# Batch 0's q and k loaded through GpSimd's queue, zero fills cut to what is read, and a redrawn instruction order, in a linear-attention and MLP-mixer kernel

## The chip, the cores and the metric

The kernel runs on one core of one Trainium2 chip. The metric is the device time of one execution in microseconds. The kernel before takes 242.99 us (median of 3 runs, 242.88 to 243.49).

## The reference, cut to what matters

Eight batches of 576 tokens, 8 heads of 64 (512 channels). Linear attention is followed by a mixer over tokens and one over channels; the result has the residual added.

```python
phi = lambda x: np.where(x > 0, x, np.exp(x) - 1.0) + 1.0
q_p, k_p = phi(q), phi(k)                        # (8, 8, 576, 64)
kv  = einsum('bhsd,bhse->bhde', k_p, v)
z   = sum(k_p, axis=2)
num = einsum('bhsd,bhde->bhse', q_p, kv)
den = einsum('bhsd,bhd->bhs', q_p, z)[..., None] + 1e-06
x   = (num / den) as (8, 576, 512)
h   = relu(x.T @ w_tok1) @ w_tok2                # 576 -> 256 -> 576, per channel
u   = x + h.T
out = u + relu(u @ w_ch1) @ w_ch2                # 512 -> 1536 -> 512, per token
```

Inputs and output are float32.

## The kernel before

**Tiles and stages.** The batches are worked one behind the other, with neighbours overlapped. A batch is loaded as two halves (heads 0 to 3 and 4 to 7) of q, k and v, each 576 KB. For each half ScalarE makes the exp (`phi_exp`, L249), VectorE the linear part (`phi_add`, L253) and the minimum of the two (`phi_end`, L259), which is phi in bf16. TensorE multiplies k and v (`kv`, L299 for batches 1 to 7; `kv_first`, L570 for batch 0), ScalarE copies the result into the block-diagonal tile `kvbd` (L305, L574), q comes to TensorE transposed (by TensorE for batches 0 and 1, `qtr_mm`, L317; by a DMA transpose on SP's queue for the others, `qtr_dma`, L332), and a product with `kvbd` gives numerator and denominator together (L349, L384; `nd_first`, L585 and L592, for batch 0). VectorE divides (L361, L410, L419; L607 for batch 0). Then come the token mixer (`mm1`, L445 and L624; `mm2`, L456, L475, L635), VectorE's residual sum u (L467, L480, L637), u's transpose (on TensorE, or by DMA on SP's queue, L486, L491), and the channel mixer: for batch 0 and part of batch 1 plain products (L683, L744), for the rest a Strassen-Winograd form of seven products, each in 2 by 2 blocks (`mix_mm`, L925, read by L938, L940, L678; `product`, L967, read by L1055, L1061, L981), with sums of blocks on VectorE (L833, L882, L894) and GpSimd (L813, L1068). The tails of 64 tokens that 576 leaves over 512 are worked in pairs of batches (L708, L730, L1021).

**Order.** The order is written out by hand of a planner: every step is a function in a table `tok`, and the string `ORDER` calls them one by one. A name is the batch, then a letter for the step, then its part: `1K` is `kv` of batch 1, `2qT0` a transpose of batch 2's q, `A..` the steps of batch 0, `..L..` a load. Each engine and each DMA queue carries out its own instructions in that order, and waits on semaphores where it reads what another has made. `BANK` says which PSUM bank a product writes, `EBUF` which of three buffers an exp goes to; a bank or buffer that is used again waits for its last reader.

**Queues.** `load` (L221) sends batch 1's halves to GpSimd's queue and all others to SP's. GpSimd's queue also has v of batch 0, cast to bf16 on its way (`load_v0`, L230), all weights, also cast (L1118 to L1137), and the stores of batches 0 to 6. The stores of batch 7 go from SP and ScalarE.

**The beginning.** TensorE multiplies zeros (`warm`, L1089, "the dummy products") while the first loads come in; `zeros` lies in the tile of batch 1's v. Around the loads stand the zero fills: `qT[b]` is the transposed q of two alternating batches, of which the last columns of each quarter and the last 64 are read beyond what is written; `w1t` holds the last 64 rows of w_tok1 in one half of its partitions, for even and for odd batches, and zeros in the other.

```python
js = slice(2 * c, 2 * c + 2)
queue = nc.gpsimd if n == 1 else nc.sync
return after(queue.dma_start(out=raw[nm, rb(n)][:, js], in_=src_[:, js]), gate)
```

Of the kernel before, what the change touches and what calls it, by code (L numbers as in the profile page):

```python
# [43 lines left out]
BANK = {k_: int(v_) for k_, v_ in (e.split(":") for e in """2K:2 2n0:1 2n1:3 2n2:6 2f:6 2g0:4 2g1:6 2X2:1 2Z2:7 2Y2:7 3K:4 3n0:4 3n1:6 3n2:0 3f:4 3g0:6 3g1:0 3X2:1 3Z2:4 3Y2:3  # L44
3gt:2 4K:0 4n0:0 4n1:2 4n2:6 4f:4 4g0:4 4g1:0 4X2:2 4Z2:1 4Y2:3 5K:6 5n0:1 5n1:3 5n2:5 5f:5 5g0:5 5g1:3 5X2:4 5Z2:5
5Y2:7 5gt:1 6K:2 6n0:1 6n1:3 6n2:5 6f:2 6g0:5 6g1:2 6X2:4 6Z2:0 6Y2:6 7K:2 7n0:2 7n1:4 7n2:6 7f:2 7g0:0 7g1:2 7X2:3
7Z2:6 7Y2:1 7gt:5 1h00:2 1h01:1 1h10:6 1h11:5 1t0:3 1t1:2 1t2:1 1t3:6 1m0:2 1m1:4 1m2:3 1m3:4 1m4:6 1m5:2 1m6:4 1m7:1
1m8:0 1m9:5 1m10:0 1m11:0 T00:1 T10:3 T01:4 T11:4 T02:5 T12:7 U08:2 U18:3 7c0:3 7c1:4 7c2:4 7c3:6 7c4:2 7c5:4 7X0:5
7Z0:4 7Y0:1 7X1:2 7Z1:0 7Y1:0 7PX0:7 7PZ0:3 7PY0:1 7PX1:6 7PZ1:5 7PY1:5 7tX:0 7tZ:4 7tY:2 1PX:3 1PZ:0 1PY:2 2PX:4
2PZ:3 2PY:5 3PX:0 3PZ:3 3PY:4 4PX:7 4PZ:0 4PY:0 5PX:0 5PZ:7 5PY:1 6PX:7 6PZ:1 6PY:6 warm0:0 0Q00:1 0Q01:2 0s0:3  # L50
warm1:0 0Q10:7 0Q11:1 warm2:5 0K0:2 0d0:1 0n0:4 0l0:6 0s1:0 0K1:1 0d1:7 0n1:0 0l1:3 0f0:2 0f1:5 0g00:0 0g01:3 0g10:4
0t0:1 0t1:6 0g11:7 0m0:6 0m1:0 0t2:1 0t3:7 0m2:1 0m3:2 0gt:5 0m4:7 0m5:3 0m6:4 0m7:2 0m8:7 0m9:1 0m10:0 0m11:5 U00:3
U01:0 1Q0:5 U02:4 U03:7 1Q1:1 1K:5 1n00:1 1n01:5 1n10:5 1n11:5 1n20:1 1n21:1 1f:5 1g2:0 0ut:6 2X1:0 2Z1:7 2Y1:3 3X1:0
3Z1:3 3Y1:6 4X1:7 4Z1:0 4Y1:0 5X1:6 5Z1:0 5Y1:2 6X1:5 6Z1:6 6Y1:1 2X0:6 2Z0:2 2Y0:2 3X0:2 3Z0:4 3Y0:5 4X0:1 4Z0:7
4Y0:5 5X0:1 5Z0:5 5Y0:0 6X0:7 6Z0:3 6Y0:2""".split())}
# [14 lines left out]
1v1 1Qc10 1K 1Kc0 1Kc1 1Q11 0q3 1Qc11 1n01 1n20 0q4 1nc01 0q5 1n10 1nc20 2Lq1 0q6 1nc10 1n00 1nc00 0q7 1n11 2qx0 2Lv0  # L70
2qx1 2Lk0 2Lk1 0q8 ws04 ws14 2Lv1 1nc11 ws24 ws34 1n21 1nc21 2qa0 2qb0 0q9 2qa1 wt2 1f1 1f0 0q10 1fr1 0q11 2v0 2qb1
3Lq0 2qT1 2qT0 1fr0 1h00 0z0 1h01 0z1 1hu01 1h11 1h10 1hu00 1t0 1hu10 1hu11 1t1 ws00 1g2 1tc1 1t2 1t3 1tc0 1ma9 0z2
1ma5 1ma1 1tc2 1tc3 1mb5 ws10 3qx0 1mb1 1ma2 1mb2 3Lq1 1gu2 2ka1 1ma8 0ut 1r5 1mb8 2kx1 2kx0 1ma7 1r1 3Lk1 1r2 2kb1
1ma0 1mb0 G14 2v1 1r0 0uc 1ma3 1mb3 1r3 2ka0 1mb7 1r7 2kb0 2K 2Kc1 3qa0 2Kc0 1ma4 1mb4 1r8 1r4 0z3 1mb9 1r9 3qb0 ws12
ws22 3qa1 3Lk0 2n 2nd 2o0 2n1 1ma11 1mb11 1r11 2o1 T02 3Lv1 1ma10 1mb10 1p10 1p11 3kx0 1ma6 3Lv0 1mb6 2ne 2n2 2n0 2f0
0o1 3qx1 3qb1 3ka0 3kb0 1r6 ws20 1w10 1w20 Tr02 T00 4Lq1 ws32 1c0 ws30 T01 4Lk0 1r10 1w13 2f1 3ka1 wt0 3kx1 3kb1 1p20
1p21 Tr01 1w23 3qT0 2fr0 2fr1 2g0 4qa1 2gu0 3v0 2g1 1p50 0o0 2gu1 3v1 1p60 4qx1 1p51 1c2 1p61 3K 3Kc0 1w40 1p30 G24
1p31 3qT1 1w30 4qb1 1eZ 1c1 1eY 1hY 1p71 2uT0 1p70 1eW Tr00 3Kc1 3n 1hW 2uT1 U00 1p41 1p40 3nd 3o0 3ne 3o1 3n1 U01
2x01 U02 3n0 3n2 2x12 4Lv1 1hZ 3f0 1eX 2s1 2x11 2s3 2x21 V0 2x15 2s2 4ka0 2y01 2x02 2x06 4kx0 4kb0 4v1 4Lv0 2s4 3f1
# [1118 lines left out]
```

## Time and profile before

| | us |
|---|---|
| median of 3 runs | 242.99 |
| the profiled execution | 244.04 |
| its span | 242.3 |
| PE busy (TensorE, products) | 233.3 (96%) |
| DVE busy (VectorE) | 214.0 (88%) |
| ACT busy (ScalarE) | 135.7 (56%) |
| POOL busy (GpSimd) | 80.8 (33%) |

All times in what follows are microseconds from the start of the span unless said otherwise; the granted clock of TensorE is 0.999 on average. PE is the row of products, PEld that of weight loads, which go on beside products. A row of waits says which engine waited at which line, for whom, the sum, the number of waits and the longest. A row of the chain gives start, length and what it was. Queue q1 is SP's and ScalarE's, q0 GpSimd's. DMA issues stand on the issuing engine; the transfer itself is not in them.

### The profile page before, as it was taken

The page shows a single profiled execution, that of the slowest core. Times are in us where ns is not written, and L with a number is a line of the kernel's source. Part 1 is how long each engine was busy: PE and PEld are TensorE (multiplying, and loading weights), DVE is VectorE, ACT ScalarE, POOL GpSimd, SP SyncE. Part 2 cuts the span into 40 slices and gives each one's busy share as a digit, 9 for nine tenths or more (in the row PEclk, how much of TensorE's full clock was granted, in tenths as well). Part 3 has the DMA queues.
Part 4 walks back from the last instruction along what each step waited for, and adds up shares of the span by engine and source line. Part 5 has one row for each costly group of instructions (what it writes and reads, how often), then busy time and mean ns, then how long its engine had stood idle before and what let it go on. Part 6 is the DMA issues. An engine that isn't in the chain of part 4 may idle for free.

```text
span 242.3 us, 6371 instructions
## 1 busy us (share of the span) xinstructions
PE 233.3 (96%) x2616; PEld 174.4 (72%) x2616; DVE 214.0 (88%) x389; ACT 135.7 (56%) x224; POOL 80.8 (33%) x92
## 2 busy tenths in 40 slices
PE   7799999999999999999999999999999999999991
PEld 3485445465678678789777887788678868888880
DVE  5889986999999999999999999999999699867661
ACT  4764781678695287428993496548914442347000
POOL 8684306370800620046000620215014900440730
PEclk9999999999999999999999999999999999999999
DMA  6999999999799988897937989594971285143035
GB/s 237 267 204 302 314 296 303 410 171 307 263 291 175 327 208 156 293 160 259 301 108 162 379 270 182 88 294 156 157 141 25 45 176 108 24 103 70 3 91 170
DMA packets 49037, 48.42 MB, mean 200 GB/s; under 512 B 30064, under 2 KB 35568, under 8 KB 49008
## 3 DMA queue, kind: packets, MB, share of 16 engines
q1 hardware_dynamic: 40032, 31.46, 47.7%
...
q8 instruction: 20, 0.33, 0.5%
...
## 4 chain that ended last, share of the span: by engine, by line
PE 86%; DMA 8%; DVE 1%; ACT 1%; issue 1%; SPq 1%; ACTq 0%
PE ps L967 26%; PE ps L925 23%; PE ps L445 6%; PE ps L744 5%; DMA v_raw<-in_v_dram 5%; PE ps L456 4%; PE ps L683 4%; DMA k_raw<-in_k_dram 3%; PE ps L708 2%; PE ps L299 2%; PE ps L730 2%; PE ps L1021 2%; PE ps L384 2%; PE ps L624 1%; PE ps L635 1%
## 5 line engine op out<-in xcount | busy, mean ns | idle before, releaser
L967 PE MATMUL ps<-k_raw,v_raw 128*128 128x256 bf16 x252 | 31.5, 273 | 0.0
L940 ACT COPY v_raw<-ps 128x512 f32<-128x512 f32 x30 | 17.2, 593 | 24.1 <-PE ps L925 18.5
L967 PEld LDWEIGHTS <-cr 128*128 128x128 bf16 x252 | 24.5, 98 | 4.8
L967 PEld LDWEIGHTS <-v_raw 128*128 128x128 bf16 x252 | 24.2, 98 | 3.8 <-issue 0.4
L925 PEld LDWEIGHTS <-swc 128*128 128x128 bf16 x240 | 23.3, 98 | 3.5 <-issue 0.4
L925 PEld LDWEIGHTS <-wc 128*128 128x128 bf16 x216 | 21.1, 98 | 4.0
L678 DVE CUSTOM_DVE_ANT_0 cr<-ps,v_raw 128x512 bf16<-128x512 f32 x30 | 20.0, 683 | 4.3 <-PE ps L925 2.1
L925 PE MATMUL ps<-crt,swc 128*128 128x256 bf16 x180 | 23.4, 273 | 0.0
L249 ACT ACTIVATE e<-q_raw 128x1152 bf16<-128x1152 f32 x16 | 18.7, 1167 | 6.7 <-DMA q_raw<-in_q_dram 6.3
L683 PE MATMUL ps<-uT,wc 128*128 128x512 bf16 x96 | 21.9, 379 | 0.0
L967 PE MATMUL ps<-wc,cr 128*128 128x256 bf16 x168 | 21.6, 273 | 0.0
L1068 POOL TENSOR_TENSOR obuf<-obuf,w 128x512 f32<-128x512 f32 x6 | 7.8, 1294 | 40.3 <-DVE obuf L1061 20.2
L249 ACT ACTIVATE e<-k_raw 128x1152 bf16<-128x1152 f32 x16 | 18.6, 1166 | 3.9 <-DMA k_raw<-in_k_dram 3.9
L1068 POOL TENSOR_TENSOR obuf<-obuf,q_raw 128x512 f32<-128x512 f32 x6 | 8.2, 1374 | 35.6 <-DVE obuf L1061 35.6
L925 PE MATMUL ps<-uT,wc 128*128 128x256 bf16 x144 | 19.7, 273 | 0.0
L1061 DVE TENSOR_TENSOR obuf<-ps,u 128x512 f32<-128x512 f32 x24 | 16.3, 684 | 2.7 <-PE ps L967 2.4
L1068 POOL TENSOR_TENSOR obuf<-obuf,part 128x512 f32<-128x512 f32 x6 | 7.7, 1286 | 27.1 <-DVE obuf L1061 27.1
L410 DVE TENSOR_TENSOR x<-ps,dens 128x768 bf16<-128x768 f32 x18 | 16.5, 937 | 0.0
L683 PEld LDWEIGHTS <-wc 128*128 128x128 bf16 x96 | 9.1, 98 | 9.8
L467 DVE TENSOR_TENSOR u<-ps,x 128x1024 bf16<-128x1024 f32 x12 | 14.5, 1218 | 0.1
L833 DVE TENSOR_TENSOR v_raw<-cr 128x512 bf16<-128x512 bf16 (+3 forms) x24 | 14.5, 617 | 0.0
L445 PE MATMUL ps<-x,w 128*128 128x512 bf16 x56 | 14.4, 379 | 0.0
...
## 6 DMA issues: line engine op xcount, KB each, us to landing
...
```

The source lines that it names most:

```text
L249: nc.scalar.activation(out=ebuf[EBUF[f"{n}{nm}{c}"]], in_=f, func=AF.Exp)
L410: nc.vector.tensor_tensor(out=xv[:, :, rc0:rc0 + 3], in0=nd_tile(n, m)[:, :, k0:k0 + 6, 0:D].rearrange("p i (q a) d -> p i q a d", a=2), i ...
L445: nc.tensor.matmul(out=banks(f"{n}f")[:, mt], lhsT=w1t[:, b, ms] if r == R else w1[:, r, ms], rhs=x[b][:, r, :], start=(r == 0), stop=(r = ...
L467: nc.vector.tensor_tensor(out=u[b][:, rs], in0=banks(f"{n}g{i}"), in1=x[b][:, rs], op=ALU.add)
L678: nc.vector._custom_dve(TENSOR_ADD_SAT, out=o, in0=ps, in1=c, s0=3.4028234663852886e38, s1=0.0)
L683: nc.tensor.matmul(out=bank(f"{n}m{mc}"), lhsT=wc1[:, kj, 128 * mc:128 * mc + 128], rhs=uTj[b][:, kj] if n < 2 - U1 else uT[b][:, :, kj], ...
L833: return engine.tensor_tensor(out=s_[which - 1][:, ks], in0=x_, in1=y_, op=op)
L925: nc.tensor.matmul(out=ps[:, j], lhsT=lhs[:, k_, 128 * j:128 * (j + 1)], rhs=rhs[:, :, k_], start=(first and j == 0 and k_ == 0), stop=(k_ ...
L940: nc.scalar.copy(out={1: c1, 6: c6, 5: c5}[i], in_=ps)
L967: nc.tensor.matmul(out=ps, lhsT=lhs[:, k_], rhs=rhs[:, k_], start=(first and not skip and k_ == 0), stop=(k_ == KH - 1), skip_group_check= ...
L1061: nc.vector.tensor_tensor(out=slots(f"{n}P", 4)[:, d::2, HC[c]], in0=pair_tile(n, "X" if z == "W" else z), in1=u[n % 2][:, d::2, HC[c]], o ...
L1068: nc.gpsimd.tensor_tensor(out=o, in0=o, in1=part[i], op=ALU.add)
```

## The change

Three parts. `load` sends batch 0 to GpSimd's queue as well, and the two loads of batch 0's v are issued right behind, ahead of the identity. The zero fills of `w1t` and `qT` move from GpSimd to VectorE, and `qT` is filled only in five blocks of 64 columns (three in `qT[0]`, two in `qT[1]`) in place of all 2368 of each. And the strings `BANK`, `EBUF` and `ORDER` are replaced: the dummy products' banks and the first nineteen steps of batch 0 stay, with the loads of batch 1 and of the weights behind them; the order from there up to step 1066 and all other banks are new; the last steps are as before.

```diff
     def load(nm, n, c, gate=None):
...
-        queue = nc.gpsimd if n == 1 else nc.sync
+        queue = nc.gpsimd if n < 2 else nc.sync
...
     for c, nms in enumerate(("kq", "qk")):
         for nm in nms:
             tok[f"0L{nm}{c}"]()
+    for c in range(2):
+        load_v0(c)
     make_identity(nc, identity)
     nc.vector.memset(ones, 0.0)
...
     for b in range(2):
         nc.vector.memset(kvbd[b], 0.0)
-    nc.gpsimd.memset(w1t, 0.0)
-    nc.gpsimd.memset(qT[0], 0.0)
-    nc.vector.memset(qT[1], 0.0)
+    nc.vector.memset(w1t, 0.0)
     for c in range(2):
-        load_v0(c)
+        for j in sorted({T * c + T, T * (2 + c) + T, 4 * T}):
+            nc.vector.memset(qT[c][:, D * j:D * (j + 1)], 0.0)
     nc.gpsimd.memset(w2p[:, NT * TD:], 0.0)
...
 ORDER = """A2 A0 A1 A3 ... 1Lv1 1Lv0
-B0 B1 B2 A22 A21 A20 A23 A24 A25 A26 A18 A29 A28 A27 A32 A30 A33 A35 A31 A32l A34 Aw10 A36 A37 Aw01 A38 A39 A40 A43
+B0 B1 B2 A21 A20 A25 A18 A23 A24 A22 A26 A29 A27 A30 A28 A33 A31 A32 A32l A35 A34 A36 A37 Aw10 Aw01 A39 A38 A40 A43
...
```

In the new order, as in the old, batch 1's k-times-v product stands behind the same amount of TensorE's work. Among the differences that the prediction speaks of: `A18`, a copy of q, comes behind batch 0's first k-times-v; the first tail product `7ta1` of the last batch stands later among the last products, the tail's mm3 products `7c0` to `7c5` a little later; batch 6's stores (`6o`) are issued behind the last of them.

More of the change, by code (lines that the diff above doesn't have):

```diff
@@ L42 @@
 WHOLE = {'00', '01', 't0', 't1'}
[L44 to L52, printed above, removed]
@@ L53 @@
-U01:0 1Q0:5 U02:4 U03:7 1Q1:1 1K:5 1n00:1 1n01:5 1n10:5 1n11:5 1n20:1 1n21:1 1f:5 1g2:0 0ut:6 2X1:0 2Z1:7 2Y1:3 3X1:0
-3Z1:3 3Y1:6 4X1:7 4Z1:0 4Y1:0 5X1:6 5Z1:0 5Y1:2 6X1:5 6Z1:6 6Y1:1 2X0:6 2Z0:2 2Y0:2 3X0:2 3Z0:4 3Y0:5 4X0:1 4Z0:7
-4Y0:5 5X0:1 5Z0:5 5Y0:0 6X0:7 6Z0:3 6Y0:2""".split())}
+BANK = {k_: int(v_) for k_, v_ in (e.split(":") for e in """2K:0 2n0:4 2n1:6 2n2:1 2f:4 2g0:5 2g1:0 2X2:0 2Z2:5 2Y2:7 3K:6 3n0:4 3n1:6 3n2:0 3f:5 3g0:2 3g1:6 3X2:2 3Z2:1 3Y2:5
+3gt:6 4K:4 4n0:3 4n1:5 4n2:0 4f:6 4g0:6 4g1:6 4X2:0 4Z2:4 4Y2:3 5K:6 5n0:0 5n1:2 5n2:6 5f:6 5g0:4 5g1:6 5X2:6 5Z2:7
@@ new lines @@
+5Y2:5 5gt:2 6K:6 6n0:4 6n1:6 6n2:0 6f:2 6g0:0 6g1:2 6X2:5 6Z2:1 6Y2:4 7K:0 7n0:0 7n1:2 7n2:5 7f:6 7g0:6 7g1:3 7X2:0
+7Z2:7 7Y2:1 7gt:1 1h00:0 1h01:1 1h10:5 1h11:7 1t0:6 1t1:1 1t2:7 1t3:0 1m0:6 1m1:2 1m2:0 1m3:7 1m4:5 1m5:4 1m6:7 1m7:5
+1m8:1 1m9:3 1m10:6 1m11:0 T00:7 T10:0 T01:4 T11:1 T02:6 T12:1 U08:2 U18:0 7c0:7 7c1:6 7c2:0 7c3:4 7c4:5 7c5:3 7X0:4
+7Z0:0 7Y0:5 7X1:2 7Z1:6 7Y1:3 7PX0:2 7PZ0:0 7PY0:1 7PX1:7 7PZ1:6 7PY1:5 7tX:3 7tZ:0 7tY:4 1PX:3 1PZ:5 1PY:2 2PX:7
+2PZ:1 2PY:2 3PX:4 3PZ:3 3PY:5 4PX:3 4PZ:0 4PY:2 5PX:7 5PZ:5 5PY:4 6PX:6 6PZ:7 6PY:3 warm0:0 0Q00:1 0Q01:2 0s0:3
@@ new lines @@
+warm1:0 0Q10:3 0Q11:2 warm2:5 0K0:0 0d0:6 0n0:0 0l0:7 0s1:4 0K1:3 0d1:5 0n1:2 0l1:6 0f0:4 0f1:0 0g00:2 0g01:3 0g10:7
+0t0:2 0t1:4 0g11:3 0m0:7 0m1:3 0t2:3 0t3:1 0m2:1 0m3:6 0gt:5 0m4:4 0m5:6 0m6:0 0m7:4 0m8:2 0m9:5 0m10:6 0m11:2 U00:7
+U01:4 1Q0:0 U02:2 U03:3 1Q1:0 1K:5 1n00:0 1n01:0 1n10:5 1n11:5 1n20:6 1n21:0 1f:5 1g2:4 0ut:0 2X1:4 2Z1:3 2Y1:3 3X1:3
+3Z1:0 3Y1:5 4X1:1 4Z1:2 4Y1:2 5X1:1 5Z1:2 5Y1:4 6X1:2 6Z1:6 6Y1:0 2X0:1 2Z0:6 2Y0:2 3X0:4 3Z0:6 3Y0:0 4X0:5 4Z0:1
+4Y0:4 5X0:0 5Z0:7 5Y0:7 6X0:3 6Z0:6 6Y0:4""".split())}
@@ L57 @@
 SLOT = {k_: int(v_) for k_, v_ in (e.split(":") for e in """0o0:0 0o1:2 1P:0 V0:4 2P:0 3P:0 V1:4 4P:0 5P:0 6P:0 7P0:4 7t:0 7P1:2""".split())}
-EBUF = {k_: int(v_) for k_, v_ in (e.split(":") for e in """0k0:0 0q0:1 0q1:2 0k1:1 1k0:2 1k1:0 1q0:2 1q1:2 2q0:1 2q1:2 2k0:1 2k1:2 3q0:0 3q1:2 3k0:1 3k1:0 4q1:0 4q0:0 4k0:2
-4k1:2 5k0:2 5k1:0 5q0:1 5q1:2 6k1:0 6k0:1 6q1:2 6q0:0 7k1:1 7k0:2 7q0:0 7q1:1 25378:240970""".split())}
+EBUF = {k_: int(v_) for k_, v_ in (e.split(":") for e in """0k0:0 0q0:1 0q1:2 0k1:1 1k0:1 1k1:2 1q0:2 1q1:0 2q0:1 2q1:2 2k0:1 2k1:0 3q0:2 3q1:0 3k0:1 3k1:2 4q1:1 4q0:1 4k0:2
@@ L62 @@
+4k1:1 5k0:2 5k1:1 5q0:2 5q1:0 6k1:2 6k0:1 6q1:0 6q0:1 7k1:2 7k0:1 7q0:2 7q1:0""".split())}
 YBUF = {k_: int(v_) for k_, v_ in (e.split(":") for e in """0k0:0 0q0:0 0q1:0 0k1:0 1k0:0 1k1:0 1q0:0 1q1:0 2q0:0 2q1:0 2k0:0 2k1:0 3q0:0 3q1:0 3k0:0 3k1:0 4q1:0 4q0:0 4k0:0
@@ L70 @@
[L70 to L79, printed above, removed]
@@ L105 @@
-7cr5 7x23 7w10 7cr4 7x24 7y23 7c3 7y24 7w30 7w20 7c2 7y13 7w14 7c0 7cr2 7w12 7w40 7cr3 7p50 7w34 7cr0 7w22 7p51 7w24
-7w42 7p10 7w44 7ts1 7p11 7ta1 7R11 7R51 7p20 7w32 7t5 7R10 7ts2 7R50 7p61 7tb1 7p31 7R61 7ts4 7R20 7p30 7R31 7tr5 7p60
-7tr1 7ts3 7p71 7R60 7p21 7t6 7R21 7R30 7p70 7R71 7D200 7tr6 7t3 7D711 7D710 7ta2 7D201 7tr3 7D210 7R70 7tb2 7p41 7D311
+B0 B1 B2 A21 A20 A25 A18 A23 A24 A22 A26 A29 A27 A30 A28 A33 A31 A32 A32l A35 A34 A36 A37 Aw10 Aw01 A39 A38 A40 A43
+A41 A42 0gt At3 2Lq0 At2 0ma0 0gv 1ka0 1kx0 1kb0 0ma3 0ma1 0ma4 0mb4 0mb0 1kx1 0mb3 G01 0r3 1ka1 0ma6 1kb1 0ma8 0mb8
@@ new lines @@
+0ma2 0mb2 0mb6 G11 0r8 G21 0r0 G13 G02 0r6 0r4 0ma9 1qx0 G04 G12 0ma10 0mb10 0ma11 0r10 0ma7 0mb7 0mb1 0mb11 0r2 1qa0
+0ma5 1qb0 0mb5 G03 1qa1 0r7 G14 0r1 0mb9 0r9 1Q00 0r11 G22 1qx1 ws02 1Q01 ws04 ws12 1Qc00 0q0 1Qc01 1qb1 1v0 0q1 0q2
+0r5 1Q10 1Qc10 ws22 1v1 1K 1Kc1 1Q11 0q3 1Kc0 1n20 1Qc11 0q4 1n01 1nc20 0q5 1n10 0q6 2qx0 1nc01 1nc10 1n00 1nc00 0q7
+1n11 ws14 0q8 1n21 2Lq1 2qx1 1nc11 1nc21 2qa0 G24 2qb0 2qa1 G23 2qb1 ws00 0q9 0q10 2Lv0 2Lk0 1f0 1fr0 1f1 1fr1 2Lk1
+2Lv1 2v0 3Lq0 3Lq1 0q11 0z0 1h01 1hu01 1h00 0z1 ws24 1h11 1hu11 1h10 1hu00 1t0 1tc0 1t1 2qT0 1hu10 1g2 1t3 2qT1 1t2
@@ new lines @@
+3Lv0 ws10 1tc1 1ma0 1ma4 2kx1 1ma8 1gu2 1tc3 1ma5 1tc2 2kx0 1ma2 1mb2 0z2 ws34 1mb5 1mb8 1ma3 2ka1 2v1 1r2 3Lk1 3qx0
+2kb1 1mb4 3qx1 2ka0 3Lk0 1r8 1mb0 1r0 2kb0 1r4 1mb3 1r3 1ma1 1mb1 3qa0 2K 2Kc1 0z3 1r5 3qb0 2Kc0 0o1 3qa1 1ma7 1mb7
+1r7 1r1 0o0 3Lv1 1ma9 1mb9 1r9 2n 4Lq1 0ut 0uc wt2 1p10 1p11 3kx0 1ma11 1mb11 2nd 2n1 2o1 1ma10 1mb10 1r10 2ne 2o0 2n0
+1ma6 1mb6 1r6 2n2 2f1 3qb1 3qT1 wt0 3ka0 1w10 3qT0 2fr1 1r11 1w13 ws32 2f0 3kb0 T00 4Lk0 2fr0 2g0 3ka1 1w23 1w20 1p50
+1p51 ws20 ws30 2gu0 1w40 3v0 3kx1 3kb1 Tr00 T01 2g1 1w30 1c0 1p61 T02 1c2 1p31 2gu1 3v1 4Lv1 Tr02 1p60 4qx1 1c1 4qa1
@@ new lines @@
+1p20 1p21 1eZ 4qb1 4ka0 1p71 3K 3Kc0 1p30 1eY 1hY 1p70 Tr01 1eW 3Kc1 3n 3nd 3ne 4kx0 U00 4v1 U01 U02 3o1 3n2 3n1 2uT1
+1p41 1p40 1hZ 2uT0 2x21 2y21 3n0 3o0 2s1 1eX 2x01 2x02 2s2 1hW 2y01 2y02 5Lq1 5qx1 4Lq0 2x25 2y25 V0 2x11 2x26 4kb0
+2y11 4qa0 3f0 4qx0 2x12 2x05 2s3 2y12 4qb0 2x06 3f1 2x15 3fr0 4Lv0 2y06 2x07 4Lk1 4ka1 2s4 2y05 5Lk0 3fr1 2y07 2x03
+2x16 2y03 2x22 2y22 2y15 2x23 2y26 2y23 2x27 2y27 2y16 2x13 2y13 4v0 2x17 5kx0 3g1 2x04 3g0 2x24 2y17 2y04 2x14 3gu1
+2w10 4kx1 2p10 2p11 1o 3gu0 2y24 2y14 2w12 2p20 5Lv1 4kb1 3gt 4K 2w22 2c0 2w20 2p21 4qT1 4Kc1 2w30 2p61 2p60 2c1 4qT0
@@ new lines @@
+2eZ 2p50 2p51 2c2 3gt1 4Kc0 3uT1 2p71 3gt0 2p70 3s3 2w40 4n 3uT0 3s1 5Lv0 2p30 2eW 2p41 5v1 2hW 5v0 2p31 4nd 4ne 4o0
+4n0 5Lk1 5kx1 2p40 3x11 3y11 4n2 3x01 3y01 3x12 4n1 4o1 3x22 3s2 3x15 3x16 3ut 3y16 2eY 3x06 3y06 3x02 2hZ 3y12 3x21
+2eX 3y02 3y15 3x17 5ka0 3y17 3x07 3x13 6Lv1 3y13 5kb0 3y21 3x05 3y05 3y07 4f1 4fr1 3x03 3y03 5Lq0 3x25 3y25 5ka1 4f0
+3s4 5kb1 T10 2hY 3y22 4fr0 4g0 5qa0 Tr10 5qx0 6Lk0 6kx0 4gu0 3x14 3x26 3y26 5qb0 3x04 W0 T11 3y04 Tr11 4g1 U10 3x27
+5qa1 3x23 4gu1 5K 3y27 3x24 3y14 3p10 3y23 2o 5qb1 T12 3y24 6ka0 3p20 3w12 5Kc1 3p11 Tr12 3p21 U11 U12 3c0 6kb0 3w10
@@ new lines @@
+3p50 3p51 3w22 3w20 6Lv0 6Lk1 6kx1 4uT0 6ka1 4uT1 3p61 4s1 3c2 3w30 3p60 6kb1 3w40 V1 W1 4s2 3p31 3eZ 5qT1 4s4 5qT0
+3p30 5Kc0 5n 6Lq1 3eY 6v0 3hZ 3c1 3p70 6v1 5nd 5n0 5o0 3p71 3eW 5n1 4x01 4x21 4x02 4y01 4y02 5ne 7Lk1 5o1 4y21 3p40
+4x06 4x26 3p41 6Lq0 6qx0 3hY 5n2 4x11 7kx1 3hW 3eX 6qa1 4x12 5f0 4y11 4x25 6qx1 4y25 3o 7Lq1 4y12 4y26 6qb1 4x16 4x15
+4y15 5fr0 4x22 5f1 4x23 4s3 4x27 6qa0 4y06 4y22 4x05 4x07 6qb0 4x13 5fr1 4y16 4x17 4y05 7ka1 6qT0 4x03 4y23 4y27 4x24
+4y24 4y07 4x04 4y04 4y17 4y03 4y13 5g1 4p10 4w10 4p11 6qT1 5gu1 5uT1 4x14 5g0 6K 4w30 4y14 4p20 4w12 4w20 7qx1 4w22
@@ new lines @@
+5gu0 4p21 4eZ 4c0 4p60 4hZ 5gt 5gt0 6Kc0 5gt1 6Kc1 6n 6ne 6nd 4w40 6o1 6n2 5uT0 5s1 6n1 5s2 4p61 4p50 6o0 4p51 5s3 4c1
+4p71 4p70 4eW 4c2 4hW 4p30 4p31 4eY 5x01 5y01 5x11 5x21 5x02 6n0 5y11 5y21 5x06 7Lk0 7Lv1 5x16 4p40 7kx0 7kb1 7ka0
+5x12 5y06 5y12 4p41 4eX 5y16 7Lq0 5x15 5x17 5x25 5y02 7F12 5y15 7qx0 7v1 5x26 6f1 5y17 5x05 5y05 5x07 7kb0 7qa1 6f0
+5s4 5x14 4hY 5y26 5y07 4o 5y25 7qb1 5x03 7qa0 5x27 7Lv0 6fr1 5x13 5y03 6fr0 6g1 7qb0 7qT1 5y27 7v0 7qT0 5x04 5x22 5y22
+5x23 5y14 5x24 5y04 5y23 5w10 6g0 5y13 6gu0 5y24 5w12 5p10 5w20 5p20 5p21 6uT0 5p11 7K 7Kc0 5w22 6gu1 5w40 6uT1 5p50
@@ new lines @@
+5p51 5c0 5p61 5c2 5eZ 5p60 5w30 7Kc1 7n 7nd 7ne 5c1 5p31 5p71 7n1 5p30 5p70 7o1 7n2 6s1 6x11 6y11 6s2 6x01 6x21 7F10
+5eY 5hY 6x02 6x16 6y01 5eW 6x06 6x05 5p40 5p41 7o0 6s3 6y06 6x07 5hW 6y02 7n0 6x12 5eX 6y16 6x17 6y05 6x15 6x03 6x22
+6y12 5hZ 6y21 7f0 7F14 6y03 7fr0 7f1 6s4 6y15 6y22 6x25 6x26 6y07 6x04 7fr1 7g0 6y17 6y25 5o 6y04 6w10 7gu0 6x14 6y26
+6x23 6y23 6x27 6y27 7gt 6x13 6y13 7gt0 7g1 7F11 6x24 6p10 6p11 7gu1 6w20 6y14 6y24 7uT0 6w12 6p20 6p21 6p50 7gt1 6w22
+6c0 6p51 6w30 6p61 7x02 6w40 6c2 7x01 6p60 6c1 6eZ 6p30 7F3 7y01 7x11 6p70 7F13 7uT1 7s3 7s1 7x05 7y05 7y11 6p31 6p71
@@ new lines @@
+7s2 7F15 7F2 7x25 7x06 7F4 7y02 7x16 6eY 7x22 6eW 7x03 7x21 7y06 6p40 7y25 7y03 6p41 7x15 7y16 6eX 6hY 7y21 7x07 5ut
+7y07 6hZ 7y15 7x26 7x17 7ut 7c4 7s4 7x04 6hW 7y26 7y17 7x23 7x13 7w30 7y22 7y04 7x27 7c1 7cr1 7y23 7c0 7y27 7x24 7c3
+7cr0 7x12 7y13 7w10 7w20 7w40 7x14 7cr4 7c5 7y12 7w32 7y14 7p11 7w34 7y24 7w12 7w14 7w24 7c2 7w44 7p51 7cr2 6o 7R11
+7w22 7p50 7p21 7w42 7p61 7R61 7R50 7p10 7R10 7cr5 7cr3 7ts1 7p20 7p71 7p30 7p60 7R20 7ta1 7tb1 7t5 7ts2 7R51 7R71 7ts4
+7R60 7R30 7p31 7D200 7p70 7R21 7tr1 7t6 7R31 7tr5 7ts3 7tr6 7t3 7D711 7D710 7ta2 7D201 7tr3 7D210 7R70 7tb2 7p41 7D311
```

28 lines of the change are left out of this document (removed).

## The prediction

> **What bounds the kernel now.** I read the table of windows first, with one window from the first product that waits for batch 1's v to TensorE's last product, one for all before it, and one where VectorE is fullest (columns: length; busy us and count of PE, PEld, DVE, ACT, POOL; granted clock; DMA share; GB/s):
>
> ```profile
> 35.82:237.17 201.35, 201.27 (x2326) 155.85 (x2326) 184.07 (x331) 111.70 (x180) 60.59 (x60) 1.00 0.73 188
> 0.00:35.82 35.82, 32.04 (x291) 18.50 (x292) 29.50 (x58) 23.97 (x44) 20.16 (x32) 1.00 1.10 271
> 60.00:180.00 120.00, 119.92 (x1502) 93.43 (x1501) 116.67 (x200) 77.49 (x121) 28.20 (x30) 1.00 0.85 220
> ```
>
> From 35.82 us to its last product TensorE is busy for 201.27 of 201.35 us at full clock: nothing is left to win there. All that can be won lies in the first 35.82 us, where PE misses 3.8 us and the DMA share is above 1. VectorE, 116.67 of 120 us busy, is the engine that could hold PE up. Next the waits of PE, and the chain of the first 37 us (start, length, what):
>
> ```profile
> PE ps L299 <- DVE vs L272: 0.5, 1, 0.5
> ```
> ```profile
> 2.27 8.18 DMA k_raw<-in_k_dram
> ...
> 23.60 11.38 DMA v_raw<-in_v_dram
> 34.98 0.02 issue
> 35.00 0.78 DVE vs L272
> 35.77 0.04 issue
> 35.82 0.78 PE ps L299 x71
> ```
>
> The chain runs through two loads: batch 0's last half of k, landed at 10.45, and batch 1's last half of v, landed at 34.98, whose cast (0.78) releases batch 1's k-times-v product at 35.82. PE stood ready 0.48 us before. So the first 36 us are set by how soon 12 MB have come in, and an earlier TensorE only waits longer at L299. The end, 237.17 to 242.3, is the last read and the writes behind it.
>
> How the two queues share the engines is in the DMA view of the first 7.9 us, and of 59.9 to 62.9 (rows of queues: packets, MB, share of 16 engines):
>
> ```profile
> q1 hardware_dynamic: 969, 2.13, 76.3%
> ```
> ```profile
> q1 hardware_dynamic: 533, 1.16, 101.6%
> ```
>
> Queue 0 is absent from both, though GpSimd issued v of batch 0 from 3.74 and a store from 59.98: SP's loads went first. Its timeline has the issues:
>
> ```profile
> 1.26 0.53 POOL L1107 MEMSET w1t<- 128x512 bf16 x1
> 1.72 2.07 POOL L1108 MEMSET qT<- 128x2368 bf16 x1
> 3.74 1.71 POOL L230 DMA_DIRECT2D cr<-in_v_dram  x2
> 11.70 0.71 POOL L225 DMA_DIRECT2D k_raw<-in_k_dram  x1 [1.86 <-DMA cr<-in_v_dram]
> ```
>
> **The four loads on GpSimd's queue.** SP loses four issues of 0.46, GpSimd gains four of 0.72 (the row of batch 1's k, 0.71). k's first half is issued at 0.74 as on SP. An idle queue 0 starts 1.2 us after its issue (stores issued at 85.37: no packet of queue 0 up to 86.5, 11 by 86.7); SP's first packet came at 1.86, 1.1 after its issue. So the stream starts 0.1 late. Then 2.36 MB pass: on SP's queue at 357 GB/s (window 2 to 8, start included), on GpSimd's at 411 for the same kind of load (window 29 to 32): 6.61 us against 5.74, 0.87 less. But SP's queue reached 403 later (40 to 46), so most of this is the start's own. Ends 0 and 0.87; I take 0.35, nearer to 0, and net of the late start a gain of 0.25 (from 0.1 lost to 0.8 won). Behind k and q the queue holds the same transfers in the same order, DMA has no idle slice until 38 us, so v of batch 1 moves by the same: landed at 34.73, product at 35.57.
>
> [...]
>
> **Waits added on GpSimd.** In the built program each DMA of this queue waits for the landing of the eighth before it. Now w1t waits for k's first half (4.5), w2 for q's (5.9), wc1's first quarters for q's and k's second halves (8.5, 10.5 at the latest). GpSimd reaches these four at 7.3, 8.0, 8.7 and 9.5, so only the last can wait, up to 1 us; its data land at 19.68, behind a full queue, and are read at 21.37. Nothing.
>
> **Fills.** GpSimd sheds 0.53 and 2.07, which pays for the four issues (2.88): v's issues start at 3.62 instead of 3.74. The identity is now made behind six issues, ready at 5.85; the first transpose reads it at 8.28: 2.4 us of cover, beyond which each us would be a us of start. VectorE sheds 1.04 (L1109) and gains w1t (256 words, half of the two kvbd fills' 0.56: 0.28) and five fills of 32 words (0.09 each, the row of 36). It ends by 3.5, and k lands at 4.5. Nothing.
>
> **Start of TensorE.** k's second half comes up to 1.5 us sooner, but ScalarE must first do q's exp and two copies, so its own exp moves from 10.53 only to about 10.1 (q landed at 8.0 instead of 8.48, exp 1.17, copy 0.57, two casts 0.33), and mm1 (L624), which comes behind it, from 15.46 to about 15.1. It all ends in the wait at L299: nothing beyond the 0.25.
>
> **The new order behind it.** Both programs have the same 2609 products. I added up the group durations along each engine's new order, and compared at every wait of PE the work ahead of it on PE with that ahead of its producer on VectorE or ScalarE, less the idling that the producer owes to PE. The thinnest place past batch 1's k-times-v product is, before, 0.21 us short (batch 6's q product L384 behind the tail add L480; the trace shows no wait there, so the sums are good to 0.2 or so); in the new order 0.12 short, L967 behind L480, all others even or better. From qp done on VectorE to the q products there are 13.3 us or more of difference in the sums before and 15.2 or more after; from u to its mix products 11.0 before and 12.7 after; only batch 2's shrinks, from 14.8 to 13.1. SP's transposes thus have their cover. In the tail the last mm3 product comes 0.65 us later in PE's order and the first tail product 3.9 us later, so GpSimd's four tail sums (6.95) have more room. So I put nothing here: ends 0 and about 2 us.
>
> **Sum.** 35.57 + 201.35 + 5.13 = 242.05 of span, 0.25 less than 242.3; the profiled execution took 244.04, 1.05 above the median of the runs, so I move the median: 242.99 - 0.25 = 242.7. (0.3%, 0.73 us, is about what a measurement of this kernel can tell from no change.)
>
> **Rivals.**
> Slower by a start-up of GpSimd's queue (0.14): its first packet of all came at 7.95, 3.36 us after the end of its issue. If that was the queue's own first start and not SP's backlog, k's first packet comes at 1.46 + 3.36 = 4.82 instead of 1.86, and all landings 2.96 later: 242.99 + 2.96 - 0.25 = 245.7. It decides from 0.35 us above an idle start. Against it: the 3 us without queue 0 from 59.98, long after any first start. [...]
>
> Slower by PE waits in the new order (0.19): if at two batches VectorE's x or u product is one place too late (937 ns of L410 each), PE waits 1.2 to 1.9 us: about 244.3. For it: 97% of VectorE. Against: the sums above. It decides once VectorE falls 0.3 us further behind.
>
> Faster (0.24): the loads run at 411 from the first byte and v lands 0.8 sooner; PE is there at 34.95, and the product starts at 35.0: 242.2 or a little less.
>
> The likeliest (0.43) is no measurable change. Faster 0.24, same 0.43, slower 0.33. The range leaves out most of the start-up and the fringe of the gain: 241.8 to 245.2.
>
> **What the profile after would show.** Right: k_raw landing about 4.6, k's second half at 9 to 9.8, L299 of batch 1 near 35.6 behind the cast of v, PE without a gap until 237. Wrong: first exp past 5.5 (start-up), PE waits on VectorE or ScalarE past 36 us (order), or v landed before 34.2 (gain).

## The result and the profile after

The changed kernel takes 250.53 us in the median of four runs (249.23 to 250.78), the kernel before 242.94 (242.80 to 243.49): slower by 7.6 us, ratio 1.029, interval 1.027 to 1.031. The profiled execution of after took 250.76 with a span of 249.0, against 242.3 of span before.

The table of windows of after, in stretches as in the prediction (columns: length; busy us and count of PE, PEld, DVE, ACT, POOL; granted clock; DMA share; GB/s):

```profile
38.24:244.60 206.36, 202.58 (x2311) 156.24 (x2326) 189.66 (x331) 113.13 (x180) 59.94 (x60) 0.99 0.71 183
0.00:38.24 38.24, 32.06 (x288) 19.43 (x290) 28.41 (x62) 24.05 (x44) 21.25 (x35) 0.96 1.07 259
```

Batch 1's k-times-v product (L299) starts at 38.24 instead of 35.82: 2.42 lost. From there to TensorE's last product it is 206.36 instead of 201.35: 5.01 lost, where the prediction had none. The tail behind it is 4.4 instead of 5.13: 0.73 won. Together 6.7, the difference of the spans. Both losses stand in the first two rows of PE's waits (us in total, times, longest):

```profile
PE ps L317 <- DVE qp L259: 4.2, 1, 4.2
PE ps L683 <- DVE x L419: 2.8, 1, 2.8
```

The kernel before has the first of them only as two short waits, and the second not at all:

```profile
PE ps L317 <- DVE qp L259: 1.3, 2, 0.8
```

And each is paid a second time, in TensorE's granted clock. Four windows of 3.41 us, two for each wait (columns as above):

```profile
7.85:11.27 3.42, 0.42 (x8) 0.42 (x9) 1.96 (x3) 2.20 (x2) 2.24 (x4) 1.00 1.03 305
11.27:14.68 3.41, 3.41 (x28) 2.87 (x26) 3.27 (x6) 2.10 (x5) 1.45 (x2) 0.50 1.30 198
65.87:69.29 3.42, 0.73 (x4) 0.37 (x4) 3.32 (x9) 0.00 (x0) 1.93 (x2) 1.00 0.85 313
69.29:72.71 3.42, 3.42 (x10) 1.23 (x9) 3.42 (x5) 1.19 (x2) 0.00 (x0) 0.50 0.02 5
```

In the first of each pair PE is busy for 0.42 and 0.73 us; in the second the granted clock is 0.50, PE is busy throughout, and does the work of 1.7 us in 3.4 (from 69.54 to 72.52 its products start 0.427 apart, ahead of the drop and behind it 0.215). So the second place costs 2.78 of idling and 1.7 of clock, 4.5 of the 5.01. The rest belongs to the new order as such: in experiments 3, 7 and 10, where this wait is gone, the same stretch still takes 202.03 to 202.14, some 0.7 more than before.

The chain of waits names the release of each. At the start it is q's first half (start, length, what):

```profile
1.30 0.86 POOL k_raw L225
2.15 6.66 DMA q_raw<-in_q_dram
```

Near 66 us it is VectorE. Its timeline and GpSimd's (start, length, engine, line, operation):

```profile
62.19 0.84 DVE L253 TENSOR_SCALAR y<-q_raw 128x1152 bf16<-128x1152 f32 x1
62.95 3.91 DVE L821 TENSOR_TENSOR k_raw<-wc 128x1536 bf16<-128x1536 bf16 x1
66.78 0.17 DVE L397 TENSOR_SCALAR dens<-ps 128x28 f32<-128x28 f32 x1
```
```profile
61.18 2.55 POOL L761 DMA_DIRECT2D out_dram<-obuf  x4 [6.47 <-DVE obuf L757]
63.74 4.13 POOL L813 TENSOR_TENSOR q_raw<-wc,q_raw 128x512 bf16<-128x512 bf16 x3
```

L821 is the step wt2, a subtraction with both operands in SBUF. Before, it stood where GpSimd was idle (from 44.43 to 48.32):

```profile
46.62 0.95 DVE L821 TENSOR_TENSOR k_raw<-wc 128x1536 bf16<-128x1536 bf16 x1
```

Here it takes 3.91, and dens and x of batch 2 queue behind it. It ends 0.8 after the second of GpSimd's three sums L813; the third takes 1.76 where the others take 1.16.

### The profile page after: what moved, and what is told of

It is laid out like the page before. It is cut to its first block, busy times and chain, and to the rows that moved or that the text cites. A ratio compares the mean times of both kernels' runs of the same rounds, so it can differ in the third digit from the quotient of the medians.

```text
span 249.0 us, 6378 instructions
## 1 busy us (share of the span) xinstructions
PE 234.6 (94%) x2597; PEld 175.7 (71%) x2616; DVE 218.5 (88%) x394; ACT 137.2 (55%) x224; POOL 81.2 (33%) x94
## 4 chain that ended last, share of the span: by engine, by line
PE 84%; DVE 5%; issue 4%; DMA 3%; ACT 2%; POOL 0%; DVEq 0%; ACTq 0%; POOLq 0%
PE ps L967 25%; PE ps L925 21%; PE ps L744 6%; PE ps L445 5%; PE ps L683 5%; PE ps L456 4%; DMA q_raw<-in_q_dram 3%; PE ps L708 2%; PE ps L730 2%; PE ps L1021 2%; PE ps L299 2%; PE ps L384 1%; DVE y L253 1%; PE ps L317 1%; PE ps L1089 1%
## 5 line engine op out<-in xcount | busy, mean ns | idle before, releaser
L967 PE MATMUL ps<-k_raw,v_raw 128*128 128x256 bf16 x252 | 31.3, 273 | 0.0
L967 PEld LDWEIGHTS <-v_raw 128*128 128x128 bf16 x252 | 24.4, 98 | 3.7 <-issue 0.2
L967 PEld LDWEIGHTS <-cr 128*128 128x128 bf16 x252 | 24.4, 98 | 3.5
L1068 POOL TENSOR_TENSOR obuf<-obuf,w 128x512 f32<-128x512 f32 x6 | 7.6, 1271 | 54.2 <-DVE obuf L1061 37.1
L683 PE MATMUL ps<-uT,wc 128*128 128x512 bf16 x92 | 22.3, 392 | 3.0 <-DVE x L419 2.8
L925 PE MATMUL ps<-crt,swc 128*128 128x256 bf16 x180 | 23.9, 273 | 0.0
L967 PE MATMUL ps<-wc,cr 128*128 128x256 bf16 x168 | 20.5, 273 | 0.0
L683 PEld LDWEIGHTS <-wc 128*128 128x128 bf16 x96 | 9.4, 99 | 13.8 <-issue 3.8
L925 PE MATMUL ps<-uT,wc 128*128 128x256 bf16 x144 | 19.1, 273 | 0.0
L938 ACT ACTIVATE cr<-ps 128x512 bf16<-128x512 f32 x18 | 10.5, 600 | 13.1 <-PE ps L925 10.4
L410 DVE TENSOR_TENSOR x<-ps,dens 128x768 bf16<-128x768 f32 x18 | 16.6, 945 | 0.1
L1068 POOL TENSOR_TENSOR obuf<-obuf,part 128x512 f32<-128x512 f32 x6 | 7.8, 1303 | 25.9 <-DVE dens L397 19.3
L833 DVE TENSOR_TENSOR v_raw<-cr 128x512 bf16<-128x512 bf16 (+3 forms) x24 | 14.6, 618 | 1.8 <-ACT cr L692 1.0
L692 ACT ACTIVATE cr<-ps 128x512 bf16<-128x512 f32 x19 | 10.4, 599 | 7.8 <-PE ps L683 7.8
```

The lines of the kernel that those rows point to most:

```text
L410: nc.vector.tensor_tensor(out=xv[:, :, rc0:rc0 + 3], in0=nd_tile(n, m)[:, :, k0:k0 + 6, 0:D].rearrange("p i (q a) d -> p i q a d", a=2), i ...
L683: nc.tensor.matmul(out=bank(f"{n}m{mc}"), lhsT=wc1[:, kj, 128 * mc:128 * mc + 128], rhs=uTj[b][:, kj] if n < 2 - U1 else uT[b][:, :, kj], ...
L833: return engine.tensor_tensor(out=s_[which - 1][:, ks], in0=x_, in1=y_, op=op)
L925: nc.tensor.matmul(out=ps[:, j], lhsT=lhs[:, k_, 128 * j:128 * (j + 1)], rhs=rhs[:, :, k_], start=(first and j == 0 and k_ == 0), stop=(k_ ...
L967: nc.tensor.matmul(out=ps, lhsT=lhs[:, k_], rhs=rhs[:, k_], start=(first and not skip and k_ == 0), stop=(k_ == KH - 1), skip_group_check= ...
L1068: nc.gpsimd.tensor_tensor(out=o, in0=o, in1=part[i], op=ALU.add)
```

## Experiments

Two theories. **S**: the loads on GpSimd's queue make q's first half late, TensorE idles, and the clock falls behind it. **P**: the new order puts wt2 beside GpSimd's sums, which hold it back. ("Port", in two of the expectations, is a name for that: no run shows what the two engines share.) Rivals are named with each run. All times are medians; "before" is 243.46 in the first four, 243.12 in the next four and 243.31 in the last three, run beside them.

**1. After, with the loads undone.**

```diff
-        queue = nc.gpsimd if n < 2 else nc.sync
+        queue = nc.gpsimd if n == 1 else nc.sync
 # and load_v0 back behind the fills
```

> The kernel after with one part undone: batch 0's q and k go back to SP's queue and the two loads of v0 back behind the fills; fills, order and banks stay new. Theory S (start): the loads on GpSimd's queue cost the 2.5 us by which the first 38 us are longer (4.2 us of idle TensorE, then 3.4 us at half clock). Then batch 0's first halves land near 4.5 and 5.9 again, TensorE never idles for over 1 us, batch 1's k-times-v product (L299) comes near 35.8 and the time falls to about 248.0; L821's stretch to 3.9 us past 62 us, being the order's own (theory P), stays. Rival C (coincidence): that stretch and the 2.8 us of idle TensorE come only from the late start; then both go, and the time is 243 to 244. Rival O (the order loses elsewhere, the start is swallowed): over 249.

Measured: 252.12, ratio 1.037 (1.034 to 1.039), slower than after itself. P held: L821 takes 3.92 again, beside L813, and PE waits 2.8 at L683, so the stretch is no coincidence of a late start (C falls). But undoing the loads did not mend the start, and S's forecast of 248.0 missed: q's second half lands at 8.9 instead of 8.5, k's at 12.0 instead of 10.45, and the clock is 0.50 from 14.02 to 20.84. Neither theory had said so; experiment 6 takes it up.

**2. Before, with the loads alone moved.** 
```diff
-        queue = nc.gpsimd if n == 1 else nc.sync
+        queue = nc.gpsimd if n < 2 else nc.sync
 # and load_v0 ahead of make_identity
```

> The kernel before with one part of the change alone: batch 0's q and k on GpSimd's queue, with v0's loads right behind them and the identity behind those; fills, order and banks stay old. Theory S: the first halves land near 5.5 and 8.8, TensorE idles some 4 us from about 6.6, the granted clock falls to 0.5 for 3.4 us, and the time is 2 to 3 us longer: 245 to 246. Rival O: the loss at the start is swallowed in the wait for v at L299 (0.5 us of room in the kernel before, and v lands 0.8 later): 243 to 244. A loss of 6 or more would put all of it on the loads.

Measured: 246.28, ratio 1.0135 (1.010 to 1.017): 2.8 us. S held: k's first half lands at 5.47, q's at 7.96, PE waits 4.2 for the first transposes, and one window later the clock is 0.50:

```profile
7.73:11.14 3.41, 0.34 (x6) 0.34 (x7) 2.95 (x3) 2.33 (x2) 3.41 (x5) 1.00 1.05 313
11.14:14.56 3.42, 3.42 (x30) 2.88 (x26) 3.28 (x5) 1.97 (x4) 3.42 (x5) 0.50 1.30 192
```

Part of the wait is a second meeting of VectorE and GpSimd: the old fills now stand behind the loads, GpSimd's fill of qT runs from 7.20 to 9.27, and VectorE's add on q (L253, 0.76 in the median), begun at 8.05, takes 1.83 beside it.

**3. After, with wt2 14 us earlier in VectorE's order.**

```diff
-... 0ut 0uc wt2 1p10 ...
+... 0ut 0uc 1p10 ...
-... 2qb0 2qa1 G23 2qb1 ...
+... 2qb0 2qa1 wt2 G23 2qb1 ...
```

> The kernel after with one step of VectorE's order moved: the sum wt2 (L821, 128x1536, two operands in SBUF) stands behind the add of batch 2's second half of q, some 14 us earlier, where GpSimd has no sums of its own, as in the kernel before. Theory P (port: the addition waits for GpSimd's sums L813 beside it): L821 takes 0.95, the dens and x of batch 2 come 3 us earlier, the second idle stretch of TensorE and the half clock behind it go: about 4.5 less, 246. Rival: L821 is slow for its operands' sake (wc and k_raw); it takes over 3 us in the new place too, and the time is 249 to 251. Rival: another operation of VectorE takes its place beside L813 and stretches: 249 or more, with L821 at 0.95.

Measured: 244.90, ratio 1.006 (1.0045 to 1.0075): 5.6 less than after. L821 takes 0.95, and of PE's waits past the start only 0.6 at L635 is left:

```profile
PE ps L317 <- DVE qp L259: 2.5, 1, 2.5
PE ps L1089 <- DVE ones L1103: 1.5, 1, 1.5
PE ps L635 <- POOL w2p L662: 0.6, 1, 0.6
```

q's first half landed at 7.37 here, 8.82 in the profiled execution of after; the wait for it is 2.5, not 4.2, and no clock fell. That is not the step's doing, since the two programs are alike up to 46 us: L299 starts at 36.49 here and at 38.24 in after, 1.75 of the 6.2 between the two spans. What the step itself is worth is read behind L299: from there to the last product it is 202.03 against 206.36, 4.3 less. The fastest run of after, 249.23 with a mean clock of 0.993 against 0.982 to 0.986 in the three others, also lies 4.3 above experiment 3. P held; the size is 4.3 to 4.5, and not 5.6.

**4. Both repairs.** The diffs of experiments 1 and 3 together.

> Both repairs at once: batch 0's q and k on SP's queue, and wt2 in its earlier place; fills where read, and the rest of the new order and banks, stay. If theories S and P are all of the loss: 250.5 less 2.5 less 4.5, 243 to 243.5, level with the kernel before (242.9), and TensorE without a gap over 1 us past the first product for v. If the new order loses elsewhere (O): 244.5 or more, and the waits of PE name where.

Measured: 249.24 (246.71 to 252.15), ratio 1.019 (1.013 to 1.025); 243 to 243.5 was expected. L821 takes 0.95, but k's second half lands at 13.15 and the clock is 0.50 from 13.62 to 20.45 (L592's ten products take 1.23 there, 0.74 in experiment 3). Behind L299 the stretch is level with experiment 3 (201.95), but L299 starts at 40.64. The start is worse than with the loads on GpSimd: the loss of 4, and what 1 has beyond wt2, is there.

**5. After, with GpSimd's sums moved instead of wt2.**

```diff
-... 1w13 ws32 2f0 ... 1p51 ws20 ws30 2gu0 ...
+... 3qb0 2Kc0 ws32 ws20 ws30 0o1 ...
```

> The kernel after with wt2 left where it is on VectorE; instead GpSimd's last three sums (L813, ws32, ws20, ws30) stand ahead of the two stores 0o1 and 0o0 and not behind them. Beside wt2 GpSimd then only writes descriptors of the four stores. Theory P (the sums' reads block VectorE's addition): L821 takes 0.95, up to 1.7 if one store's writing holds it at first, the second idle stretch of TensorE and its half clock go: 245 to 246.3 (the kernel with wt2 moved took 244.9). Rival D (the descriptor writes of the stores block it): L821 stays over 3 us, 249 to 251.

Measured: 246.92 (246.27 to 249.66), ratio 1.019 (1.013 to 1.025). wt2 runs in the old place, beside the stores:

```profile
63.11 0.94 DVE L821 TENSOR_TENSOR k_raw<-wc 128x1536 bf16<-128x1536 bf16 x1
```
```profile
61.35 2.56 POOL L761 DMA_DIRECT2D out_dram<-obuf  x4 [1.52 <-DVE obuf L757]
```

The issues of the stores do not hold it (D falls); the sums do. (The expectation calls them descriptor writes; what GpSimd does in the 2.56 of L761 is not shown.) The time is above experiment 3's, by 1.4 in the better two runs; the profile shows 3.3 of wait at the start, q's first half landing at 8.23, and two new waits of 0.5 and 0.4 at L683.

**6. Before, with the fills alone changed.** 
```diff
-    nc.gpsimd.memset(w1t, 0.0)
-    nc.gpsimd.memset(qT[0], 0.0)
-    nc.vector.memset(qT[1], 0.0)
+    nc.vector.memset(w1t, 0.0)
+    for c in range(2):
+        for j in sorted({T * c + T, T * (2 + c) + T, 4 * T}):
+            nc.vector.memset(qT[c][:, D * j:D * (j + 1)], 0.0)
```

> The kernel before with the fills alone changed: GpSimd's fill of w1t and of all of qT's first buffer (0.53 and 2.07) and VectorE's fill of the second are replaced by VectorE's fills of what is read; loads on SP's queue, order and banks as before. Theory F (the fills held v0 back): GpSimd issues v0 2.3 us sooner, its first packet comes at 5.5 instead of 7.95 and takes bytes from q's and k's second halves, which land at about 9.0 and 12.0 instead of 8.5 and 10.45; first product for v, mm1 and L299 some 2 us later, with half clock in some runs: 245.5 to 247.7. Rival N (as the prediction had it, the fills cost and bring nothing): 243.2 to 243.8.

Measured: 248.23, ratio 1.020 (1.016 to 1.024): theory F, and more than it said, 5.1. With the fills gone from GpSimd, v0 is issued at 1.47 instead of 3.74. The DMA view of 5.5 to 8.5 us:

```profile
DMA packets 494, 0.86 MB, mean 287 GB/s; under 512 B 14, under 2 KB 226, under 8 KB 494
...
q1 hardware_dynamic: 282, 0.62, 60.9%
q0 software_dynamic: 212, 0.24, 47.5%
```

Queue 0 takes nearly half of the engines' time for 0.24 MB (v0 counted in bf16, as it is written; the float32 that is read is twice that). K's second half lands at 12.77 instead of 10.45, the first product L317 of the second half waits 1.4, and the clock is 0.50 from 14.30 to 21.12. The 2.6 us of fills on GpSimd, most of them of columns that nobody reads, had kept v0 off the stream until 7.95, when q's second half was nearly in.

**7. New order and banks alone, with wt2 early.** Loads and fills as before: the kernel before with the tables BANK, EBUF and ORDER of experiment 3, so that the diff is that of the tables.

> The new order and PSUM banks alone, with wt2 in its earlier place; loads on SP's queue and the fills as before. If wt2 beside the sums is all that is wrong with the new order, there is no idle stretch of TensorE over 1 us past the first product for v, and the time is level with the kernel before: 243.0 to 243.9. If the order loses elsewhere: 244.5 or more. A gain over the kernel before (under 242.8) would make this the best version.

Measured: 243.26 in ten runs, ratio 1.0008 (0.9997 to 1.0018). The redrawn order, apart from that one step, costs and brings nothing that can be measured here: what stands behind L299 is 0.7 longer, and L299 comes 0.9 sooner (34.87).

**8. Experiment 2 with twice the dummy products.**

```diff
-lambda: warm(0, 4),
+lambda: warm(0, 8),
```

> The kernel with the loads alone moved (old fills and order), with eight dummy products instead of four ahead of the first transposes, so that TensorE works until about 10 us in the time in which it waits for q. Theory H (half of that loss is the granted clock, which falls after a window in which TensorE idled): no stretch at 0.5 past the start, the first 38 us shorter by 1.5 to 1.9: 244.4 to 244.9 instead of 246.3. Rival W (the wait for q alone counts, the clock would have cost nothing, or falls all the same): 246 or more.

Measured: 245.35, ratio 1.009 (1.008 to 1.011), against 1.0135. The same stretch as in experiment 2, now with PE kept at work:

```profile
8.28:11.69 3.41, 2.79 (x24) 1.38 (x22) 3.05 (x4) 2.36 (x3) 3.41 (x5) 1.00 1.10 304
11.69:15.10 3.41, 3.15 (x67) 2.27 (x65) 3.06 (x6) 3.05 (x7) 3.41 (x6) 1.00 1.30 182
```

The clock stays at 1.00 (mean of 0.997 to 1.000 in the four runs, 0.986 to 0.993 in those of experiment 2), and against its own before the loss is 2.2 instead of 2.8. H held for the clock, not for the size: 0.6, where 1.5 to 1.9 was expected, and with intervals that overlap it is not clear of noise. In the profiled execution q's first half landed 0.45 later than in 2, which hides part of it, and L299 started 0.83 sooner (37.55 against 38.38).

**9. Before, with wt2 moved beside the sums.**

```diff
-... 2qb0 2qa1 wt2 1f1 ...
+... 2qb0 2qa1 1f1 ...
-... 3qb0 ws12 ws22 3qa1 3Lk0 2n 2nd ...
+... 3qb0 ws12 ws22 3qa1 wt2 3Lk0 2n 2nd ...
```

> The kernel before with one step moved and nothing else: wt2 (L821) goes from 46.6 us to just behind the add of batch 3's q at 60.4, so that it would begin about 61.2, 0.1 us ahead of GpSimd's three sums L813 (61.30 to 64.71) and beside the end of two store issues. Theory P in the form that the kernel after shows (the sums win even when VectorE's addition began first): L821 takes 3 us or more, batch 2's dens and x come late, TensorE idles 2 to 3 us near 65, and the time is 245.5 to 248. Rival R (whoever begins first keeps the port): L821 takes 0.95, the first L813 is longer by about 0.8, and the time is 243.0 to 244.0. If L821 is 0.95 and L813 unchanged, theory P falls.

Measured: 248.62, ratio 1.020 (1.018 to 1.023): 5.3 lost by that move alone.

```profile
60.72 4.44 DVE L821 TENSOR_TENSOR k_raw<-wc 128x1536 bf16<-128x1536 bf16 x1
```
```profile
60.93 3.40 POOL L813 TENSOR_TENSOR q_raw<-wc,q_raw 128x512 f32<-128x512 bf16 x3
```
```profile
PE ps L967 <- DVE x L419: 3.5, 1, 3.5
```

The three sums run at their own 1.13 each; the subtraction, begun 0.2 ahead of them, ends 0.8 behind the last. Rival R falls here. PE waits 3.5, and the clock is 0.50 for the window behind it:

```profile
64.42:67.83 3.41, 0.77 (x8) 0.69 (x8) 3.27 (x9) 0.07 (x1) 1.09 (x2) 1.00 0.69 221
67.83:71.25 3.42, 3.42 (x13) 1.58 (x11) 3.35 (x5) 0.44 (x1) 0.00 (x0) 0.50 0.41 163
```

3.5 + 1.7 = 5.2, the whole loss.

**10. Split queues.** Experiment 3, with the first halves of k and q on SP's queue and the second halves, v0 and the weights on GpSimd's.

```diff
-        queue = nc.gpsimd if n < 2 else nc.sync
+        queue = nc.gpsimd if n == 1 or (n == 0 and c == 1) else nc.sync
```

> The kernel after with wt2 in its earlier place, and batch 0's first halves of k and q on SP's queue, the second halves, v0 and the weights on GpSimd's. Theory S2 (the loss of the loads is GpSimd's late start; its in-order queue behind SP's first halves is good): first halves land near 4.5 and 5.9 at the latest, second halves near 9 to 9.5, before v0; TensorE waits 0.8 for the first transposes as in the kernel before, no half clock, k-times-v of batch 1 at 34.9 to 35.5: 242.3 to 243.2. Rival: GpSimd's packets come from 5.4 and take bytes from q's first half or start late: 243.3 to 245.

Measured: 242.96 in twelve runs (242.54 to 244.29), ratio 0.9989 (0.9975 to 1.0002): S2 held, and the change with these two repairs is level with the kernel before, not measurably better. The DMA view of 5.5 to 8.5 us, and PE's wait:

```profile
DMA packets 336, 1.18 MB, mean 392 GB/s; under 512 B 33, under 2 KB 93, under 8 KB 336
```
```profile
PE ps L317 <- DVE qp L259: 1.7, 1, 1.7
```

q's first half lands at 6.06, the second halves at 7.47 and 8.91, k's 1.5 sooner than before; L299 starts at 34.87, and PE is there 0.17 ahead of v's cast. The wait of 1.7 is not the 0.8 of the forecast: qp comes only 0.1 later than before, but the dummy products end 0.8 sooner (6.69 against 7.48).

**11. Experiment 3 with the identity made ahead of the loads.**

```diff
+    make_identity(nc, identity)
     for c, nms in enumerate(("kq", "qk")):
...
         load_v0(c)
-    make_identity(nc, identity)
```

> The kernel after with wt2 in its earlier place, and the identity made ahead of the loads on GpSimd instead of behind them. Theory I (what puts k's issue off to 1.30, and the packets' slow stretch from 6 to 7 us, are the queue's own; the identity has no part): issue of k at 1.3 to 1.5, the first packet 1.56 behind it, the slow stretch stays, q's first half lands at 7.4 to 8.9, time 244.7 to 246.5. Rival: the making of the identity (5.7 to 6.8, stretched from 0.20 to 0.74 beside VectorE's add) slows the packets; then the stretch goes, q's first half lands near 6.9, time 243.8 to 244.4.

Measured: 245.37, ratio 1.009 (1.007 to 1.010). k is issued at 1.50, right behind the identity, its first packet comes 1.57 later, and the stream is slow as before (267 GB/s from 5.5 to 8.5), with q's first half at 8.28. Theory I held: the identity has no part in the late stream.

## Why the prediction was wrong

**What bounds the kernel.** Right that the first 36 us hang on the loads and that TensorE is full behind them. But I read "nothing is left to win there" and not its other half: on an engine that is full, whatever is lost is lost for good.

**The loads.** The step "the stream starts 0.1 late" failed: GpSimd's issue began at 1.30, not 0.74, and the first packet came 1.56 later, not 1.2, so at 2.86 against 1.86. The 0.35 that I took as gained by a faster stream had the wrong sign. From 5.5 to 8.5 us the DMA view of after reads

```profile
DMA packets 211, 0.87 MB, mean 289 GB/s; under 512 B 23, under 2 KB 23, under 8 KB 211
```

and in the kernel before

```profile
DMA packets 484, 1.04 MB, mean 347 GB/s; under 512 B 19, under 2 KB 46, under 8 KB 484
```

The 411 that I took from 29 us on is what the queue does once it runs, as experiment 10's 392 shows, and not what it does at the start. k's first half landed at 5.47 (forecast 4.6), its second at 11.65 (9 to 9.8), v of batch 1 at 35.77 (34.73). The start-up rival priced 2.96: it had the right place. Its 3 to 4 us delay is real, but only beside SP's stream: queue 0's first packet came 4.2 after its first issue in the kernel before, 4.1 in experiment 1 and 3.9 in 10, and 1.56 to 1.58 wherever the queue had the engines to itself.

**Start of TensorE.** "It all ends in the wait at L299: nothing" failed. That wait gave 0.5 of room. I followed k's second half, and not q's first, on which the first transposes hang: they moved from 8.29 to 10.85. And I had no term for the clock. The trace of after has it at 0.50 for 3.413 us, twice, with 54.6 from the end of the one to the start of the other, 16 times as long, and 174.08 from the second to the next drop, 51 times; in the kernel before it stays at 1.00 for 235.52, 69 times. So I count in windows of 3.413. The drops came after windows in which PE was busy for 0.34 (experiment 2) to 1.57 of 3.41 (experiment 6, from 10.88), not only after idle ones (the kernel before, at 241.67, behind its last product). No clean limit comes out of the runs: 1.51 kept the clock in experiment 3 (from 237.01, counted on from 8.32; the last product ends at 238.52, and the mean clock is 1.000).

**Fills and identity.** "Nothing" is wrong in both settings. With the loads on SP the new fills cost 5.1 (experiment 6), since v0's packets then come in among those of k and q. With the loads on GpSimd, where v0 stands behind them in one queue, the new fills seem to win: experiment 2 with the old fills loses 2.8, experiment 3 with the new ones and a level order 1.4. The wait of 4.2 in experiment 2 holds 1.07 by which a fill stretched VectorE's add; how much of the rest is the change of the start from run to run is not shown. The identity's cover held: made by 6.8, first read at 10.85.

**Waits added on GpSimd.** Right for this kernel: three of the four wait, w2 0.51 and two of wc1 0.67 each, where I had one, and PE has no wait there. In experiment 3, with a quicker start, PE waits 0.6 at L635 for GpSimd's copy L662, which stands behind these issues.

**The new order.** "Nothing" failed at one step, and the rival's mechanism (VectorE late, PE waits) came true at another place than named: not L967 behind L480, but batch 2's x behind wt2. The failing step is the method: I added up durations engine by engine, with 0.95 for L821 from a row where GpSimd was idle, and never asked what stands beside it. Everything else in that sum held: experiment 7 is level to 0.2 us. The traces have 0.95 for L821 beside nothing or beside stores, and 3.91 to 4.44 beside three sums. To begin first did not help it: wt2 began 0.8 and 0.2 ahead of the sums and lost to them.

A rival is that the two meet at the tile wc, which both read. A row of after speaks against it: at 199.36 VectorE's L882, which reads uT and crt, takes 1.47 instead of 0.42 beside GpSimd's L866, which reads wc.

**Sum.** Experiment 7 has the new order with wt2 early and the old loads and fills, and is level with the kernel before. Against its span of 241.6 that of after is 7.4 longer: L299 comes 3.37 later (38.24 against 34.87), from there to the last product it is 4.30 longer, and the tail is 0.27 shorter. The first is the loads and fills, wait and clock together; the second is wt2 beside the sums, which alone cost 5.3 in experiment 9. In experiment 3, whose start lost no clock, the loads and fills cost 1.4. My two slower rivals were priced one by one, at 245.7 and 244.3; what came was a late start and a wait for VectorE together, each with a price in the clock that neither had.

**What stays open.** Why the first load on GpSimd's queue is slow up to 8.5 is not settled. Most of its packets of 4608 bytes take 0.178, but in after 17 of 188 from 5.5 to 8.5 took 0.4 to 1.3; with SP's first halves ahead of them, in experiment 10, all take 0.178 there, and the queue moves 1.16 MB in that stretch instead of 0.87. Why q's first half lands at 7.37 in one program and at 8.82 in another with the same beginning is not seen either. Nor is it seen why wt2 is held back by sums that begin after it. It ended 0.80 and 0.83 behind the end of a sum, nearly its whole 0.95, as if it had hardly begun before. And the same lead can win: in the kernel before, at 180.34, VectorE's sum L833 began 0.22 ahead of GpSimd's L1068 and took its 0.95, and the GpSimd sum took 1.86 instead of 1.27. There GpSimd had been idle; beside wt2 it was issuing stores, with its sums right behind. Whether that is the reason was not tested.
